# Hash attention and a two-layer MLP: the last quarter of the weight conversion beside the first batch's MLP, the sums product between the halves of the v product, the division in two parts

## The chip, the cores and the metric

The kernel runs on one core of a Trainium2 chip. The metric is the device time of one execution in microseconds (us); each version is judged by the median of several runs. The engines are TensorE (PE; its weight loads are listed as PEld), VectorE (DVE), ScalarE (ACT), GpSimd (POOL) and SyncE (SP), whose queue starts nearly all transfers.

## The reference

The first half is attention with a hash mask, over 4 batches, 8 heads, 768 positions and 64 numbers a head; the second half is an MLP over the 3072 tokens that come out, with 512 to 2048 to 512 features and a leaky activation whose slope `alpha` belongs to the feature.

```python
q_bits = (np.einsum('bhsd,dk->bhsk', q, proj) > 0)      # 6 bits
k_bits = (np.einsum('bhsd,dk->bhsk', k, proj) > 0)
mask = q_bucket[:, :, :, None] == k_bucket[:, :, None, :]
scores = np.where(mask, scale * np.matmul(q, k.transpose(0, 1, 3, 2)), -1e9)
attn = np.exp(scores - np.max(scores, axis=-1, keepdims=True))
attn = attn / (np.sum(attn, axis=-1, keepdims=True) + 1e-09)
x = np.matmul(attn, v)           # then (B,H,S,D) -> (B*S, H*D)
h = x @ w_in
g = np.maximum(h, 0.0) + alpha * np.minimum(h, 0.0)
return g @ w_out
```

The weights come in as 64-bit floats; the kernel rebuilds each one as a 32-bit float from its high and low word.

## The kernel before, in words

`fast_path` does the work; `general_path` behind it is only entered if a flag, worked out in `verdict` from the largest magnitudes seen, says that the fast way was not safe. Every compute instruction goes through `do`, which keeps the order of the program on each engine, so the order in which the code calls its helpers is the order on the queues. Transfers are issued by `nc.sync` and stand on the queue where their waits come due in that order.

**Attention.** Two heads make a pair, so there are 16 pairs; each pair's 768 queries are two units of 384 (CW) columns, so there are 32 units. The unit loop is at L871. In unit u the code calls `scores` three times (parts 0, 1, 2; each makes two blocks of 128 keys by 384 queries for both heads on TensorE, and ScalarE's exponential puts them into one of ten `pt` buffers, L653 and L658). Between the parts stands the work of other stages:

- the sums over keys of unit u: GpSimd adds the first three key blocks (`add_first` L667, `add_third` L670), VectorE the last three and the total (`add_last` L674 to L676, called one unit later);
- the v product of unit u-1 in two halves (`attend`, L686), after parts 0 and 1;
- the sums product of unit u-1 (`totals`, L698): a product with a matrix of ones, which spreads the sum of `accd`. Before the change it follows the second half of the v product. Its output lies in one of the two "mi" banks of PSUM, which the transposes of q and k (`turn`, L614) and the hash (`hash_bits`, L636) use as well;
- the division of unit u-1 (`divide`, L708 to L713), after part 2: a transpose of the sums on VectorE, a reciprocal of the 12 columns that matter, a transpose back, and the product with the v result, which is then stored to `x_s` in DRAM.

**Weight conversion.** 32 pieces (NW) of 128 x 512 numbers, the first 16 (HW) of w_in, the others of w_out. Before, unit u converts piece u. `weight_abs` (ScalarE, L546) is called at the end of the unit before, `weight_parts` (four VectorE operations, L552, L553, L556, L557) after the first half of the v product, `weight_sum` (L577, L582) and `weight_group` after part 1. The group closes four pieces of w_in or two of w_out: four differences on VectorE (L599) that the MLP's scheme needs, and the transfer of the seven blocks to `w_in_s` or `w_out_s` in DRAM. `load_weight` brings the pieces in, three ahead.

**MLP.** Both layers use a scheme with 7 products in place of 8 for a 2 x 2 split (class `Product`). A block of the first layer (`ff1`, 8 a batch) has 7 products of 4 matmuls; a block of the second (`ff2`, 3 a batch) 7 of 16. Each `step` issues one product into a bank "a", "b" or "c"; `keep` has ScalarE copy a partial result out of the bank (tiles `p1`, `p5`, `u1`, `u2`), and `finish` adds two partial results on VectorE (L798) and applies the activation (L803), or for the quadrant "21" copies on ScalarE into `h` and applies it. After "21" of a first-layer block four sums of activations are made (L810), one each for `g` 3, 5, 4 and 6. The order of steps is written out at L937 to L956: 2, 22, 5, 6, 3, 7 of a block, then step 1 of the next, then step 4 of this one. In the profile f_2a is bank a of block 2 of the first layer, z_0b bank b of block 0 of the second.

The differences of the MLP's input, `sums_x` (four GpSimd subtractions of 768 columns, L732), for the first batch are called in unit 16 (HW). `verdict` (small VectorE reductions and four transposes on TensorE, L839 to L853) stands after block 2 of the first batch. The second layer's weights come back from DRAM in the first batch's first-layer blocks, one `wo` tile a block.

Of the kernel before, what the change touches and what calls it, by code (L numbers as in the profile page):

```python
# [403 lines left out]
def fast_path(  # L404
# [71 lines left out]
    prob, accp, accd, av, vsum, sums = {}, {}, {}, {}, {}, {}  # L476
# [40 lines left out]
    HW = NW // 2  # L517

# [12 lines left out]
    def load_weight(i):  # L531
        if i < NW:
            raw[i] = pool.tile([P, 512], moe_w_in.dtype, name=f"raw{i}", tag="raw", bufs=3)
            nc.sync.dma_start(raw[i], piece(i))
# [8 lines left out]
    def weight_abs(i):  # L543
        lo, hi = halves(i)
        wx[i] = pool.tile([P, 512], F32, name=f"wx{i}", tag="wx")
        do(ACT.activation(wx[i], hi.bitcast(F32), AF.Abs))  # L546

    def weight_parts(i):
        lo, hi = halves(i)
        x = wx[i]  # L550
        wr[i] = r = pool.tile([P, 512], F32, name=f"wr{i}", tag="wr", bufs=1)
# [4 lines left out]
        do(DVE.tensor_scalar(r.bitcast(U32), x.bitcast(U32), 0x7F800000, None, op0=ALU.bitwise_and))  # L556
        do(DVE.scalar_tensor_tensor(r, lo, 2.0 ** -52, r, op0=ALU.mult, op1=ALU.mult))  # L557

    def weight_sum(i):
# [26 lines left out]
    def weight_group(i):  # L586
# [113 lines left out]
    def divide(u):  # L700
# [6 lines left out]
        d = pool.tile([P, CW], F32, name=f"dn{u}", tag="dn", bufs=1)  # L707
# [32 lines left out]
    class Product:  # L740
# [20 lines left out]
        def keep(self, bank, what):  # L761
            t = mid.tile([P, CW], F32, name=f"{self.name}{what}", tag=what)[:, : self.width]
# [28 lines left out]
    def ff1(b, i):  # L791
        def finish(c, t, more):
            if more is None:
                h = mid.tile([P, CW], F32, name=f"h{b}_{i}", tag="h")
# [9 lines left out]
            if c == "21":  # L804
                for to, x, op, y in (
# [4 lines left out]
                    do(DVE.tensor_tensor(g_m[to, i], g_m[x, i], g_m[y, i], op=op))  # L810
# [6 lines left out]
    def ff2(b, t):  # L817
        o = {}

        def finish(c, x, more):  # L820
            ch, half = int(c[0]) - 1, slice((int(c[1]) - 1) * DM // 2, int(c[1]) * DM // 2)
            if ch not in o:
                o[ch] = late[0].tile([P, DM], F32, name=f"o{b}_{t}_{ch}", tag=f"o{ch}")
# [45 lines left out]
    for i in range(3):  # L869
        load_weight(i)  # L870
    for u in range(UNITS):  # L871
        pi, g = divmod(u, NCH)
        more = pi + 1 < NPAIR
        scores(u, 0)
        add_first(u)
        if u == 0:
# [24 lines left out]
        if u > 0:  # L901
            attend(u - 1, 1)
            totals(u - 1)
# [3 lines left out]
        if u > 0:  # L907
            divide(u - 1)
        load_weight(u + 3)
        if u == HW:  # L910
# [4 lines left out]
        if u + 1 < NW:  # L915
            weight_abs(u + 1)
# [11 lines left out]
    add_last(last)  # L928
    attend(last, 1)
    now.step(5)  # L930
    totals(last)
    divide(last)
    attn.close()
    late.append(ctx.enter_context(tc.tile_pool(name="late", bufs=2)))
    blocks = [(b, what, n) for b in range(B) for what, count in (("1", NI), ("2", CH)) for n in range(count)]

    for j, (b, what, n) in enumerate(blocks):  # L937
        for st in ((2, 22, 6, 3, 7) if j == 0 else (2, 22, 5, 6, 3, 7)):
            now.step(st)
# [9 lines left out]
        if j == 2:  # L949
            verdict()  # L950
# [35 lines left out]
```

## Time and profile before

| | us |
|---|---|
| runs before | 997.28, 998.04, 999.90 |
| median | 998.04 |
| the profiled execution, its own time | 1000.19 |
| its span, first to last instruction | 998.3 |
| TensorE busy in it | 963.2 (96%) |
| VectorE busy | 605.8 (61%) |
| ScalarE busy | 371.0 (37%) |
| GpSimd busy | 158.5 (16%) |
| mean granted TensorE clock | 0.994 |

The profile is of one execution. A page shows, among others, the span in 40 equal slices of 25 us with each engine's busy share in tenths; the instructions grouped by source line, with the number of instructions, the mean duration in ns and the idle time before them; and who waited for whom ("A <- B: total us, times, longest us"). The stretches give each engine's busy time with its number of instructions between two times, then the granted clock, the share of the transfer engines and GB/s. A row of the timeline has start, duration, engine, line, operation, output and inputs, shape and count; in brackets stands the idle time before it with what ended it. Some durations that the prediction uses, from the groups:

| line | what | count | mean ns |
|---|---|---|---|
| L674, L675, L676 | VectorE's additions for the sums, 768 columns | 32 each | 1260, 1364, 1667 |
| L667, L670 | GpSimd's additions, 768 columns | 32 each | 1939, 1946 |
| L732 | GpSimd's differences of the input, 768 columns | 16 | 2005 |
| L553 | VectorE, shift and exclusive or of a piece | 32 | 1149 |
| L577, L582 | VectorE, the two last operations of a piece | 32 each | 867, 781 |
| L599 | VectorE, differences of a group: w_in, w_out | 16, 32 | 691, 425 |
| L803 | VectorE, activation from h | 32 | 692 |
| L810 | VectorE, sums of activations, 384 columns | 128 | 665 |

### The profile page before, as it was taken

To read this page: it belongs to the slowest core of one execution; us is meant where nothing else is said; L and a number is where in the kernel's file an instruction comes from. 1 tells how busy PE (TensorE), PEld (TensorE's weight loads), DVE (VectorE), ACT (ScalarE), POOL (GpSimd) and SP (SyncE) were. 2 spreads that over 40 slices of the span, in tenths; PEclk is the share of its full clock that TensorE was granted. 3 is DMA by queue.
4 is the path that set the end of the run, shared out by engine and by line. 5 is a ranking of instruction groups with operands and counts; after the bars stand their busy time and mean duration, and the time that the engine had idled before them with its cause. 6 is when DMAs were issued, how large, how long until landed. Compare 5 with 4: busy or idle time off the path is not lost.

```text
span 998.3 us, 12489 instructions
## 1 busy us (share of the span) xinstructions
PE 963.2 (96%) x4741; PEld 594.0 (60%) x4741; DVE 605.8 (61%) x959; ACT 371.0 (37%) x669; POOL 158.5 (16%) x98
## 2 busy tenths in 40 slices
PE   6999999989999998999999999999999999999997
PEld 3444444434444443455788655888656888556886
DVE  3999999999999999766600366500467300665100
ACT  6777676665777664222100122100222000222000
POOL 2333333262333333000300000300000300000000
PEclk9999999998999999999999999999999999999999
DMA  7465756355444431463400133300224200231000
GB/s 199 126 182 143 237 154 179 107 164 157 143 143 143 127 111 53 200 259 110 137 22 22 58 111 99 123 22 21 71 88 155 68 22 22 84 111 37 22 22 24
DMA packets 93316, 106.81 MB, mean 107 GB/s; under 512 B 53296, under 2 KB 79936, under 8 KB 93248
## 3 DMA queue, kind: packets, MB, share of 16 engines
q1 hardware_dynamic: 91680, 105.54, 33.1%
q8 instruction: 39, 0.64, 0.3%
q10 hardware_dynamic: 1568, 0.39, 0.2%
q14 instruction: 29, 0.24, 0.1%
HBM read 78.65 MB, written 27.26 MB: 106 GB/s over the span
## 4 chain that ended last, share of the span: by engine, by line
PE 61%; DVE 35%; ACT 1%; issue 1%; DMA 1%; DVEq 0%; SPq 0%; ACTq 0%
PE z_2a L756 6%; PE z_1a L756 6%; PE z_0a L756 6%; DVE accd L676 5%; DVE accd L675 4%; DVE accd L674 4%; DVE wx L553 3%; PE z_1c L756 3%; PE z_0c L756 3%; PE z_2c L756 3%; DVE wr L577 2%; DVE wr L557 2%; PE f_2a L756 2%; PE f_3a L756 2%; PE f_7a L756 2%; PE f_6a L756 2%
## 5 line engine op out<-in xcount | busy, mean ns | idle before, releaser
L658 ACT ACTIVATE pt<-sc 128x768 f32<-128x768 f32 x192 | 149.9, 813 | 119.8 <-PE sc L653 119.8
L653 PE MATMUL sc<-qT,kT 64*128 64x384 f32 x768 | 157.5, 487 | 0.0
L686 PE MATMUL av<-pt,vn 128*64 128x385 f32 (+1 forms) x768 | 138.1, 495 | 0.0
L667 POOL TENSOR_TENSOR accp<-pt,pt 128x768 f32<-128x768 f32 x32 | 62.0, 1939 | 222.5 <-ACT pt L658 185.2
L686 PEld LDWEIGHTS av<-pt,vn 128*64 128x64 f32 x768 | 49.4, 136 | 72.6 <-issue 72.6
L732 POOL TENSOR_TENSOR x<-x,x 128x768 f32<-128x768 f32 x16 | 31.9, 2005 | 364.0 <-DMA x<-x_s 363.4
L810 DVE TENSOR_TENSOR g<-g,g 128x384 f32<-128x384 f32 x128 | 82.5, 665 | 2.2
L653 PEld LDWEIGHTS sc<-qT,kT 64*128 64x128 f32 x768 | 69.8, 190 | 15.3 <-issue 15.2
L653 PEld LDWEIGHTS <-kb 64*128 64x128 bf16 x384 | 24.4, 94 | 79.3 <-issue 62.7
L653 PE MATMUL sc<-qb,kb 64*128 64x384 bf16 x384 | 64.6, 329 | 5.6 <-ACT pt L658 5.6
L670 POOL TENSOR_TENSOR accp<-accp,pt 128x768 f32<-128x768 f32 x32 | 62.3, 1946 | 39.0 <-ACT pt L658 38.9
L756 PE MATMUL z_2a<-wo,g 128*128 128x256 f32 x256 | 58.0, 379 | 0.5 <-ACT z_2u L763 0.5
L756 PE MATMUL z_1a<-wo,g 128*128 128x256 f32 x256 | 57.9, 379 | 0.0
L756 PE MATMUL z_0a<-wo,g 128*128 128x256 f32 x256 | 57.9, 379 | 0.0
L676 DVE TENSOR_TENSOR accd<-accd,accp 128x768 f32<-128x768 f32 x32 | 53.4, 1667 | 3.3
L803 DVE SCALAR_TENSOR_TENSOR g<-h,alpha 128x384 f32<-128x384 f32 x32 | 22.1, 692 | 54.4 <-ACT h L795 54.4
L756 PEld LDWEIGHTS z_2a<-wo,g 128*128 128x128 f32 x256 | 48.6, 190 | 8.1 <-ACT z_2u L763 0.9
L756 PEld LDWEIGHTS z_0a<-wo,g 128*128 128x128 f32 x256 | 48.6, 190 | 7.5
L756 PEld LDWEIGHTS z_1a<-wo,g 128*128 128x128 f32 x256 | 48.6, 190 | 6.6
L675 DVE TENSOR_TENSOR accd<-accd,pt 128x768 f32<-128x768 f32 x32 | 43.7, 1364 | 3.3
L674 DVE TENSOR_TENSOR accd<-pt,pt 128x768 f32<-128x768 f32 x32 | 40.3, 1260 | 0.0
L639 ACT ACTIVATE qb<-hs,hb 32x384 bf16<-32x384 f32 x64 | 36.7, 574 | 2.2 <-PE hs L636 1.0
(217 smaller groups left out, 1477.1 us busy)
## 6 DMA issues: line engine op xcount, KB each, us to landing
wi<-w_in_s SPq DMA_DIRECT2D x32, 896.0 KB, 4.6
raw<-in_moe_w_in_dram SPq DMA_DIRECT2D x16, 512.0 KB, 4.1
raw<-in_moe_w_out_dram SPq DMA_DIRECT2D x16, 512.0 KB, 3.6
w_in_s<-wsi SPq DMA_DIRECT2D x16, 448.0 KB, 5.4
w_out_s<-wso SPq DMA_DIRECT2D x8, 896.0 KB, 4.4
wo<-w_out_s SPq DMA_DIRECT2D x8, 896.0 KB, 7.4
qn<-in_q_dram SPq DMA_DIRECT2D x32, 192.0 KB, 3.7
vn<-in_v_dram SPq DMA_DIRECT2D x16, 384.0 KB, 4.4
```

Source lines behind the costliest of these rows:

```text
L639: do(ACT.activation(bits["q", pi][D * s : D * s + 32, cols], ps[r], AF.Sign, bias=hb[r]))
L653: do(PE.matmul(sc[:, s, :CW], what["k", pi][r, ks], what["q", pi][r, qs], start=first, stop=not first,))
L658: do(ACT.activation(pt[:, :, :CW], sc[:, :, :CW], AF.Exp, scale=SCALE / DOWN))
L667: do(POOL.tensor_tensor(accp[u], p(u, 0), p(u, 1), op=ALU.add))
L670: do(POOL.tensor_tensor(accp[u], accp[u], p(u, 2), op=ALU.add))
L674: do(DVE.tensor_tensor(accd[u], p(u, 3), p(u, 4), op=ALU.add))
L675: do(DVE.tensor_tensor(accd[u], accd[u], p(u, 5), op=ALU.add))
L676: do(DVE.tensor_tensor(accd[u], accd[u], accp[u], op=ALU.add))
L686: do(PE.matmul(av[u][D * s : D * s + D, :w], nat["v", pi][:, s, kc * D : (kc + 1) * D], prob[u, kc][:, s, :w], start=(kc == 0), stop=(kc = ...
L732: do(POOL.tensor_tensor(x_m[b, to], x_m[b, a], x_m[b, c], op=ALU.subtract))
L756: do(PE.matmul(self.ps[bank], self.left(left, k), self.right(right, k), start=start and k == 0, stop=k == self.nk - 1, skip_group_check=no ...
L810: do(DVE.tensor_tensor(g_m[to, i], g_m[x, i], g_m[y, i], op=op))
```

## The change

- **Conversion.** Pieces 0 to 23 (LW) are converted in attention, in three units of four: unit u takes piece u - u//4 if u % 4 < 3, and every fourth unit takes none. Pieces 24 to 31 are converted one in each first-layer block of the first batch, after that block's step 7; their results (the second half of w_out) go straight into the tiles `wo` 4 to 7 and not through DRAM. `weight_abs` is called in the same unit as the rest, after part 0. The tiles of a piece come from another pool (`mid`), with two `raw` buffers in place of three and one `wx` in place of two; `load_weight` runs two pieces ahead and is called after the group.
- **Sums product.** `totals` is called after the first half of the v product and before part 1 of the scores.
- **Division.** `divide` keeps the transposes and the reciprocal, and is called after `add_third`, before `weight_sum`. The product with the v result and its store become `finish`, called after the second half of the v product.
- **Sums of activations.** In the first batch the four sums of each first-layer block are made by GpSimd in place of VectorE.
- **The rest.** The first batch's `load_x` and `sums_x` move from unit 16 to unit 26; `verdict` moves from after block 2 to after block 8, the first of the second layer; `p5`, `u2`, `h`, `o` and `wso` have one buffer in place of two; the eight `wo` tiles are made at once when the attention's pool is closed.

The core of the diff:

```diff
+    LW = NW - NI
...
             if m == 0:
-                wst[HW + n] = pool.tile([P, NM, DM // 2], F32, name=f"wso{n}", tag="wso")
+                wst[HW + n] = (
+                    pool.tile([P, NM, DM // 2], F32, name=f"wso{n}", tag="wso", bufs=1) if n < NI // 2 else wo[n]
+                )
...
-        else:
+        elif n < NI // 2:
             nc.sync.dma_start(w_out_s[n], w)
...
         do(DVE.transpose(d, r.unsqueeze(2).to_broadcast([P, CW // 32, 32])))
+
+    def finish(u):
+        pi, g = divmod(u, NCH)
+        b, hp = pairs[pi]
         x = pool.tile([P, CW], F32, name=f"x{u}", tag="x")
-        do(DVE.scalar_tensor_tensor(x, av[u][:, :CW], vsum[pi], d, op0=ALU.add, op1=ALU.mult))
+        do(DVE.scalar_tensor_tensor(x, av[u][:, :CW], vsum[pi], den[u], op0=ALU.add, op1=ALU.mult))
         nc.sync.dma_start(x_s[b, hp][:, g * CW : (g + 1) * CW], x)
...
-            t = mid.tile([P, CW], F32, name=f"{self.name}{what}", tag=what)[:, : self.width]
+            t = mid.tile([P, CW], F32, name=f"{self.name}{what}", tag=what, bufs=2 if what in ("p1", "u1") else 1)[:, : self.width]
...
-                    do(DVE.tensor_tensor(g_m[to, i], g_m[x, i], g_m[y, i], op=op))
+
+                    do((DVE if b else POOL).tensor_tensor(g_m[to, i], g_m[x, i], g_m[y, i], op=op))
...
+        w = u - u // 4 if u % 4 < 3 else NW
         scores(u, 0)
         add_first(u)
+        if w < LW and w > 0:
+            weight_abs(w)
...
         if u > 0:
             attend(u - 1, 0)
-        weight_parts(u)
+            totals(u - 1)
+        if w < LW:
+            weight_parts(w)
         scores(u, 1)
         add_third(u)
-        weight_sum(u)
-        weight_group(u)
+        if u > 0:
+            divide(u - 1)
+        if w < LW:
+            weight_sum(w)
+            weight_group(w)
+            load_weight(w + 2)
...
             attend(u - 1, 1)
-            totals(u - 1)
+            finish(u - 1)
...
         scores(u, 2)
-        if u > 0:
-            divide(u - 1)
-        load_weight(u + 3)
-        if u == HW:
+        if u == UNITS - 6:
             load_w(0)
             load_w(1)
             load_x(0)
             sums_x(0)
-        if u + 1 < NW:
-            weight_abs(u + 1)
...
     add_last(last)
+    totals(last)
     attend(last, 1)
     now.step(5)
-    totals(last)
     divide(last)
+    finish(last)
     attn.close()
     late.append(ctx.enter_context(tc.tile_pool(name="late", bufs=2)))
+    wo += [late[0].tile([P, NM, DM // 2], F32, name=f"wo{n}", bufs=1) for n in range(NI)]
...
             if b == 0:
-                wo.append(late[0].tile([P, NM, DM // 2], F32, name=f"wo{n}", bufs=1))
-                nc.sync.dma_start(wo[n], w_out_s[n])
+                if n < NI // 2:
+                    nc.sync.dma_start(wo[n], w_out_s[n])
+                weight_abs(LW + n)
+                weight_parts(LW + n)
+                weight_sum(LW + n)
+                weight_group(LW + n)
+                load_weight(LW + n + 2)
...
-        if j == 2:
+        if j == NI:
             verdict()
```

More of the change, by code (lines that the diff above doesn't have):

```diff
@@ L475, in fast_path @@
     nat, tr, bits = {}, {}, {}
-    prob, accp, accd, av, vsum, sums = {}, {}, {}, {}, {}, {}
+    prob, accp, accd, av, vsum, sums, den = {}, {}, {}, {}, {}, {}, {}
     def load(pi, name, queue=None):
@@ L532, in load_weight @@
         if i < NW:
-            raw[i] = pool.tile([P, 512], moe_w_in.dtype, name=f"raw{i}", tag="raw", bufs=3)
+            raw[i] = mid.tile([P, 512], moe_w_in.dtype, name=f"raw{i}", tag="raw")
             nc.sync.dma_start(raw[i], piece(i))
@@ L544, in weight_abs @@
         lo, hi = halves(i)
-        wx[i] = pool.tile([P, 512], F32, name=f"wx{i}", tag="wx")
+        wx[i] = mid.tile([P, 512], F32, name=f"wx{i}", tag="wx", bufs=1)
         do(ACT.activation(wx[i], hi.bitcast(F32), AF.Abs))
@@ L550, in weight_parts @@
         x = wx[i]
-        wr[i] = r = pool.tile([P, 512], F32, name=f"wr{i}", tag="wr", bufs=1)
+        wr[i] = r = mid.tile([P, 512], F32, name=f"wr{i}", tag="wr", bufs=1)
         do(DVE.tensor_scalar(x, x, HI_MIN, None, op0=ALU.max, op1=ALU.max, accum_out=wmax[:, i : i + 1]))
@@ L706, in divide @@
         r = pool.tile([P, CW // 32], F32, name=f"rc{u}", tag="rc")
-        d = pool.tile([P, CW], F32, name=f"dn{u}", tag="dn", bufs=1)
+        den[u] = d = pool.tile([P, CW], F32, name=f"dn{u}", tag="dn", bufs=1)
         do(DVE.transpose(a, sums[u]))
@@ L793, in finish @@
             if more is None:
-                h = mid.tile([P, CW], F32, name=f"h{b}_{i}", tag="h")
+                h = mid.tile([P, CW], F32, name=f"h{b}_{i}", tag="h", bufs=1)
                 do(ACT.copy(h, t))
@@ L822, in finish @@
             if ch not in o:
-                o[ch] = late[0].tile([P, DM], F32, name=f"o{b}_{t}_{ch}", tag=f"o{ch}")
+                o[ch] = late[0].tile([P, DM], F32, name=f"o{b}_{t}_{ch}", tag=f"o{ch}", bufs=1)
             if more is None:
@@ L868, in fast_path @@
     load(1, "v")
-    for i in range(3):
+    for i in range(2):
         load_weight(i)
```

## The prediction

> **What bounds the kernel now.** I read the page's slices first, then the stretches of the two stages, TensorE's waits, and last the timeline around its longest wait.
>
> ```profile
> PE   6999999989999998999999999999999999999997
> DVE  3999999999999999766600366500467300665100
> POOL 2333333262333333000300000300000300000000
> ```
> TensorE is full everywhere; VectorE is full only in the first sixteen slices, the attention stage.
>
> ```profile
> core 0: us, PE busy (x) PEld busy (x) DVE busy (x) ACT busy (x) POOL busy (x), PEclk, DMA share, GB/s
> 0.00:409.58 409.58, 383.66 (x2505) 169.32 (x2505) 374.65 (x552) 272.96 (x451) 134.84 (x86) 0.99 0.49 147
> 409.58:558.09 148.51, 146.28 (x563) 106.69 (x562) 62.70 (x116) 23.90 (x53) 7.90 (x4) 0.99 0.33 120
> 558.09:702.85 144.76, 144.76 (x561) 106.40 (x561) 57.93 (x97) 24.76 (x55) 7.89 (x4) 1.00 0.22 73
> ```
> Attention, the first batch's MLP, the second's. A batch whose TensorE never idles takes 144.76 us, so the MLP is TensorE's alone. In attention both engines look full, but TensorE hardly waits for VectorE:
>
> ```profile
> PE sm L698 <- DVE accd L676: 7.7, 6, 3.0
> ...
> PE tp_q L614 <- DVE st L708: 2.7, 6, 0.6
> ```
> That makes attention TensorE's too, with VectorE just behind. I measured it by the start of each unit's first score product: 21.74, 33.53, 45.35 us and so on, 11.79 and 11.83 in turn, whenever nothing waits. From unit 1 to the first product after attention is 409.58 - 21.74 = 387.84 us. The floor is 29 units x 11.81 = 342.5, 10.25 for unit 30 (no transposes left; 12.50 less its gaps) and 18.0 for unit 31 and the tail (20.53 less gaps): 370.7. So all of VectorE's load in attention costs 17.1 us, the most that this change can win there: 0.8 in each of units 8, 12 and 16 (a group of four differences), 5.6 in unit 17, 0.7 in 18, 3.7 over units 20 to 28, 2.2 in unit 30, 2.5 in the tail, about 17. The largest piece is this one:
>
> ```profile
> 210.37 8.39 POOL L732 TENSOR_TENSOR x<-x,x 128x768 f32<-128x768 f32 x4
> ...
> 210.73 1.92 DVE L556 TENSOR_SCALAR wr<-wx 128x512 uint32<-128x512 uint32 x1
> 212.68 2.19 DVE L557 SCALAR_TENSOR_TENSOR wr<-raw,wr 128x512 f32<-128x512 uint32 x1
> 214.90 2.19 DVE L577 SCALAR_TENSOR_TENSOR wr<-wx,wr 128x512 f32<-128x512 f32 x1
> ...
> 225.84 1.55 PE L698 MATMUL sm<-accd,ones 128*64 128x384 f32 x4 [3.04 <-DVE accd L676]
> ```
> Four GpSimd subtractions run in a row, and each VectorE operation beside them takes 1.9 to 2.2 us where it takes 0.43 or 0.69 alone: one waits about 1.5 us per GpSimd operation, in turn. The lag reaches TensorE's sums product, which waits 3.04 us.
>
> **What the Trainium skill says.** "SBUF — State Buffer", section "Who interferes with whom": a VectorE operation with two SBUF inputs, or in a 2-port mode, is locked out while GpSimd reads SBUF, and the other way round; one with a single SBUF input, or a tensor_scalar that writes its accumulator, is not. The trace agrees: L577, 0.69 alone, takes 2.06 to 2.19 beside GpSimd; L552 (accumulator) and L713 (one PSUM input) never stretch. "GPSIMD Engine Reference", in the table that reconciles its model with measured numbers: a two-input fp32 add of 2048 columns takes 4497 ns, 2.2 ns a column; 768 columns take 1.81 us here when nothing is in the way, 2.4 a column. "TensorE: Matmul & The Clock Gate", Part 1: the clock is halved after a mostly idle window of 3.4 us. Here the 3.04 us wait brought clock 0.5 for 6.8 us, the 1.97 us wait of the verdict 3.4 us.
>
> **The change, attention.** One unit in four now converts no piece. VectorE's own work per unit, from uncontended rows: three additions 3.0 us, division 1.7, product x 0.53: 5.2. A piece is 3.83 (225.61 to 229.44), a group 2.66 for w_in (103.88 to 106.54), 1.72 for w_out. Before, four units hold 4 x (5.2 + 3.83) + 2.66 = 38.8, and last 48.04: waits for GpSimd's two additions add about 2.2 a unit. After: 4 x 5.2 + 3 x 3.83 + 0.75 x 2.66 + 8.8 = 43.1, against 47.2 of TensorE. On average VectorE has 4 us to spare.
>
> But the sums product moves forward from about +9.1 us in the unit to +4.6 (where scores part 1 starts now), and needs the three additions done. The last exponential lands near +0.8, so they end at +2.9 if VectorE is on time: 1.7 us of slack. A plain converting unit (5.2 + 3.83 + 2.2 = 11.2) keeps that. A unit with a w_in group does not: laying the rows end to end, x ends at +13.4, the next additions start at +1.6 and one meets GpSimd's first addition (+3.5): ready at +6.1, TensorE waits 1.5. There are four such units (4, 9, 14, 20): 6.0 us. Behind a w_out group x ends near +12.5 and the additions at +3.8: nothing. The burst of four subtractions moves to unit 26, and now hits L582 and all three additions: ready near +7.0 in unit 27, 2.4 us of wait and about 1 for the clock (3.4 us at half speed is 1.7, taken at just over half a chance). Unit 30 (group, but only 10.2 us of TensorE) leaves unit 31 2.1 us. With 0.5 for the rest, 12 of the 17.1 us stay: attention gains 5. Bounds: gain 12 if the group units catch up unseen, none if contention falls on the additions everywhere.
>
> **The change, first MLP.** TensorE needs 9.03 us a block. VectorE loses the four sums L810 (0.55 each) to GpSimd. It keeps three additions at 0.59 from start to start and four activations at 0.53: 3.89; a piece adds 3.83, a group every second block 0.86 on average: 8.58. That would fit. But GpSimd's four sums of 384 columns read SBUF just there: three can start as soon as the activation of "22" is done, which is when the piece starts. No row shows 384 columns. Half of the 1.5 us is 0.75 per operation; the price above gives 0.84 in all; below nothing is excluded, since a lock only takes time. Laid out: 0.3 on L553 (the first sum hides mostly behind L552), 0.7 on L556, 0.7 on L557, and 0.4 for the fourth sum on the next block's activation: 2.1 a block (bounds 0.9 and 3.0). VectorE then needs 10.7 us a block against 9.03 and is the bound. From the first product after attention: first addition of "22" at 5.75, eight blocks of 8.58 less the 2.24 of a next block, plus 16.4: the last activation of ff1, behind piece 31 and its group, ends at 88.6. TensorE wants it for the end of z_0b, at 76.1. Loss 12.5 us. TensorE runs at most half a block ahead of VectorE (p5, u2, h have one buffer), so about 6 us of it fall together before z_0b: a clock drop, +2. Sum +14.5.
>
> Costed at nothing: single buffers for p5, u2, h, o in later batches (p5 is free 1.8 us after a block's last product and needed 5.2 after; o's copy-out of 2.0 us has over 13); the SP queue (a raw load waits for L582, but stands behind the wi load that is due; wi's load of 4.6 us has 7 before its block, 1.4 in the lagging state; if that goes, the rest of the 4.6 appears per block); ScalarE's Abs, moved behind two exponentials (it hides beside the additions); w_out of four pieces no longer passing through DRAM. The verdict's wait moves from after block 2 to after z_0: it cost 4.8 us including the clock, and I leave it so, +-2.
>
> Sum: -5 + 14.5 = +9.5. The profiled execution (span 998.3, its own time 1000.19) would become 1009.7; the median of the runs, 998.04, is 2.15 below it: 1007.5.
>
> **Rivals.** (1) Attention wins nearly everything (12 us) while the MLP still loses 14.5: 1000.5. For it: VectorE's 4 us to spare in four units. Against: TensorE's new deadline half a unit earlier. (2) The other side, faster: GpSimd's sums fall beside operations that don't contend (L552, the PSUM additions), at 0.9 us a block. VectorE needs 9.5; the loss is 3.1 with no clock drop, and attention gains 10: 991. The loss is 7.8 times the wait a block less 3.9: with attention's gain at 5 the sign turns at 1.1 us a block, with 10 at 1.8. Against: the burst at 210 us, where each operation waited in turn. (3) Worse: 3.0 a block (loss 20, clock 3) and no gain in attention: 1021. That the change does not do what it says I exclude: in the instruction streams of the changed program the sums product stands between the halves, and 24 pieces stand in attention.
>
> **Chances.** Forecast 1003 to 1014: 0.55; (1) 0.15; (2) 0.15; (3) 0.15. A measurement can tell 0.3%, 3 us. Faster (below 995): most of (2) and a little of (1), 0.17. Same: the rest of (1), 0.13. Slower: 0.70. Range: 992 to 1018, cutting the far halves of (2) and (3).
>
> **What would show it.** The changed profile should have: unit starts 11.8 apart except after units 4, 9, 14, 20 (sums product waiting for accd about 1.5) and in unit 27; ff1 blocks of the first batch over 10 us with VectorE full; L553, L556, L557 stretched there; a wait of several us in z_0b for the activation; later batches at 144.8. I am wrong if GpSimd's 384-column sums leave L556 and L557 at 0.43 and 0.69, or if the sums product waits in every unit.

## The result, and the profile after

| | before | after |
|---|---|---|
| runs, us | 997.28 to 999.90 (4) | 1012.92 to 1015.51 (4) |
| median, us | 997.95 | 1014.01 |
| the profiled execution, its own time | 1000.19 | 1015.51 |
| its span | 998.3 | 1013.7 |
| mean granted TensorE clock | 0.994 | 0.991 |

The changed kernel is slower: the ratio is 1.0159, with a 95% interval of 1.0138 to 1.0179. In the line numbers of the changed kernel the sums product is L701, its input is made at L677 to L679, GpSimd's additions are L670 and L673, the differences of the input L739; the operations of a piece are L553, L554, L557, L558, L580, L585 and its group L602; the division is L711 to L714 and L720; the MLP's products are L763, the copies out of a bank L770, the additions L805, the activation L810 and the sums of activations L818.

The same three rows of slices as before, now of the changed kernel:

```profile
PE   6999989999999898999699999999999999999997
...
DVE  3777777876968787799710166600366400565100
...
POOL 2322322232232632243510000300000300000000
```

VectorE is less busy in attention than it was (mostly 7 and 8 tenths where it had 9), and TensorE has lost a little more there all the same. VectorE's 9s now stand in slices 18 and 19, the first batch's first layer; TensorE has 9s there too, and a 6 in slice 20, where the second layer begins.

The stretches of attention (from unit 1), of the first batch's MLP and of the second's say how much:

```profile
core 0: us, PE busy (x) PEld busy (x) DVE busy (x) ACT busy (x) POOL busy (x), PEclk, DMA share, GB/s
22.27:412.79 390.52, 370.95 (x2429) 162.91 (x2428) 304.91 (x466) 254.99 (x417) 122.43 (x66) 0.99 0.45 127
412.79:573.57 160.78, 149.03 (x562) 107.15 (x561) 87.81 (x151) 28.77 (x62) 40.64 (x36) 0.98 0.31 108
573.57:718.33 144.76, 144.76 (x562) 106.40 (x561) 57.80 (x97) 24.70 (x55) 7.90 (x4) 1.00 0.22 73
```

Attention takes 390.52 us against 387.84 before (+2.7), the first MLP, from its first product behind attention to the same product of the next batch, 160.78 against 148.35 (+12.4), the second batch 144.76 as before. With 0.5 us before unit 1 and -0.2 at the end that is the 15.4 us by which the span grew. TensorE's waits in the changed kernel (total, times, longest):

```profile
PE sm L701 <- DVE accd L679: 14.4, 6, 4.4
...
PE z_0b L763 <- DVE g L810: 5.0, 1, 5.0
PE f_7c L763 <- ACT f_7p L770: 2.2, 1, 2.2
...
PE f_5c L763 <- ACT f_5p L770: 1.2, 1, 1.2
PE vd L852 <- DVE top L847: 1.1, 1, 1.1
```

Six waits of the sums product, 14.4 us, stand where the kernel before had six of 7.7 in all. They lie in units 5, 10, 15, 21 (behind a group of w_in), 27 (behind the four subtractions) and 31; every other unit from 1 to 29 is 11.79 or 11.83 long, except 12.23 for unit 26, and unit 30, which has no transposes, takes 10.22. The wait of z_0b for the activation is new. A half-clock stretch of 3.41 us lies in unit 10, and two longer ones follow the two longest waits (the clock is the last column but two):

```profile
core 0: us, PE busy (x) PEld busy (x) DVE busy (x) ACT busy (x) POOL busy (x), PEclk, DMA share, GB/s
346.44:353.27 6.83, 5.07 (x20) 1.95 (x24) 3.27 (x5) 0.97 (x2) 1.63 (x2) 0.50 0.00 0
500.04:506.87 6.83, 5.75 (x14) 4.59 (x15) 1.41 (x4) 0.00 (x0) 5.59 (x4) 0.50 0.00 0
```

TensorE worked 5.07 and 5.75 us of them at half speed, so by estimate half of that, 2.5 and 2.9 us, is lost on top of the waits.

**The longest unit.** VectorE around the four subtractions in unit 26 and the start of unit 27 (339.12), then GpSimd, then TensorE:

```profile
334.57 1.61 DVE L712 TENSOR_SCALAR rc<-st 128x12 f32<-128x12 f32 x1
...
336.98 1.49 DVE L580 SCALAR_TENSOR_TENSOR wr<-wx,wr 128x512 f32<-128x512 f32 x1
338.51 2.18 DVE L585 SCALAR_TENSOR_TENSOR wso<-raw,wr 128x512 uint32<-128x512 uint32 x1
...
341.14 2.05 DVE L677 TENSOR_TENSOR accd<-pt,pt 128x768 f32<-128x768 f32 x1
343.29 2.38 DVE L678 TENSOR_TENSOR accd<-accd,pt 128x768 f32<-128x768 f32 x1
345.78 2.37 DVE L679 TENSOR_TENSOR accd<-accd,accp 128x768 f32<-128x768 f32 x1
```
```profile
334.47 1.68 POOL L673 TENSOR_TENSOR accp<-accp,pt 128x768 f32<-128x768 f32 x1 [1.90 <-ACT pt L661]
336.10 8.75 POOL L739 TENSOR_TENSOR x<-x,x 128x768 f32<-128x768 f32 x4
344.82 2.51 POOL L670 TENSOR_TENSOR accp<-pt,pt 128x768 f32<-128x768 f32 x1
```
```profile
348.20 1.55 PE L701 MATMUL sm<-accd,ones 128*64 128x384 f32 x4 [4.42 <-DVE accd L679]
```

GpSimd has six operations in a row without a gap, from 334.47 to 347.33, and VectorE six two-input or tensor_scalar operations beside them, each 0.8 to 1.5 us longer than alone (0.69 for L580 and L585, 0.96 for an addition). Even L712, a tensor_scalar of 12 columns that takes 0.17 us alone, took 1.61. The last addition ends 9.0 us into unit 27, and TensorE's sums product starts right behind it.

**The first layer of the first batch.** VectorE in block 3, between two pieces of the conversion:

```profile
441.20 0.68 DVE L553 TENSOR_SCALAR_CACHE_REDUCE wx<-wx 128x512 f32<-128x512 f32 x1
...
441.93 0.72 DVE L554 TENSOR_SCALAR wx<-wx 128x512 uint32<-128x512 uint32 x1
442.68 1.10 DVE L557 TENSOR_SCALAR wr<-wx 128x512 uint32<-128x512 uint32 x1
443.82 1.37 DVE L558 SCALAR_TENSOR_TENSOR wr<-raw,wr 128x512 f32<-128x512 uint32 x1
445.22 0.69 DVE L580 SCALAR_TENSOR_TENSOR wr<-wx,wr 128x512 f32<-128x512 f32 x1
...
447.67 1.06 DVE L810 SCALAR_TENSOR_TENSOR g<-f_3p,alpha 128x384 f32<-128x384 f32 x1
...
450.88 0.68 DVE L553 TENSOR_SCALAR_CACHE_REDUCE wx<-wx 128x512 f32<-128x512 f32 x1
...
462.40 0.68 DVE L553 TENSOR_SCALAR_CACHE_REDUCE wx<-wx 128x512 f32<-128x512 f32 x1
```
```profile
441.37 3.27 POOL L818 TENSOR_TENSOR g<-g,g 128x384 f32<-128x384 f32 x3 [2.74 <-DVE g L810]
447.31 1.00 POOL L818 TENSOR_TENSOR g<-g,g 128x384 f32<-128x384 f32 x1 [2.67 <-DVE g L810]
```

From one L553 to the next are 9.68 us without a group, and 11.52 in the following block, which has one. VectorE has no gap in either, and TensorE needs 9.03 a block. L554, L557, L558 and one activation are 0.29, 0.67, 0.68 and 0.44 us longer than alone: 2.1 a block, while GpSimd's four sums run.

### The profile page after: what moved, and what is told of

Same layout as the page of the kernel before. It is cut to its first block, busy times and chain, and to the rows that moved or that the text cites. A ratio compares the mean times of both kernels' runs of the same rounds, so it can differ in the third digit from the quotient of the medians.

```text
span 1013.7 us, 12460 instructions
## 1 busy us (share of the span) xinstructions
PE 966.1 (95%) x4741; PEld 595.4 (59%) x4741; DVE 566.9 (56%) x927; ACT 371.7 (37%) x669; POOL 184.9 (18%) x130
## 4 chain that ended last, share of the span: by engine, by line
PE 77%; DVE 15%; ACT 5%; issue 3%; DMA 1%; SPq 0%; ACTq 0%; DVEq 0%
PE sc L656 10%; PE av L689 9%; PE z_2a L763 5%; PE z_1a L763 5%; PE z_0a L763 5%; ACT pt L661 3%; PE z_0c L763 3%; PE z_2c L763 3%; PE z_1c L763 3%; PE hs L639 2%; PE f_0a L763 2%; PE sm L701 2%; PE f_5a L763 2%; PE f_6a L763 2%; PE f_7a L763 2%
## 5 line engine op out<-in xcount | busy, mean ns | idle before, releaser
L670 POOL TENSOR_TENSOR accp<-pt,pt 128x768 f32<-128x768 f32 x32 | 63.6, 1986 | 187.9 <-ACT pt L661 187.9
L739 POOL TENSOR_TENSOR x<-x,x 128x768 f32<-128x768 f32 x16 | 31.6, 1983 | 275.3 <-DMA x<-x_s 274.6
L673 POOL TENSOR_TENSOR accp<-accp,pt 128x768 f32<-128x768 f32 x32 | 54.0, 1688 | 86.2 <-ACT pt L661 79.3
L818 DVE TENSOR_TENSOR g<-g,g 128x384 f32<-128x384 f32 x96 | 60.7, 653 | 1.7
L763 PE MATMUL z_0a<-wo,g 128*128 128x256 f32 x256 | 58.1, 379 | 1.0 <-DVE g L810 1.0
L763 PE MATMUL z_2a<-wo,g 128*128 128x256 f32 x256 | 58.0, 379 | 0.5 <-ACT z_2u L770 0.5
L763 PE MATMUL z_1a<-wo,g 128*128 128x256 f32 x256 | 57.9, 379 | 0.0
L763 PEld LDWEIGHTS z_0a<-wo,g 128*128 128x128 f32 x256 | 48.6, 190 | 8.8 <-DVE g L810 1.4
L763 PEld LDWEIGHTS z_2a<-wo,g 128*128 128x128 f32 x256 | 48.6, 190 | 8.1 <-ACT z_2u L770 0.9
L763 PEld LDWEIGHTS z_1a<-wo,g 128*128 128x128 f32 x256 | 48.6, 190 | 6.6
L818 POOL TENSOR_TENSOR g<-g,g 128x384 f32<-128x384 f32 x32 | 33.5, 1056 | 65.4 <-DVE g L810 47.9
L677 DVE TENSOR_TENSOR accd<-pt,pt 128x768 f32<-128x768 f32 x32 | 31.7, 989 | 20.2 <-ACT pt L661 20.2
L580 DVE SCALAR_TENSOR_TENSOR wr<-wx,wr 128x512 f32<-128x512 f32 x32 | 42.2, 1319 | 0.3
L810 DVE SCALAR_TENSOR_TENSOR g<-h,alpha 128x384 f32<-128x384 f32 x32 | 20.5, 641 | 38.3 <-ACT h L802 38.3
L701 PE MATMUL sm<-accd,ones 128*64 128x384 f32 x128 | 27.1, 503 | 14.4 <-DVE accd L679 14.4
```

Source lines behind the costliest of these rows:

```text
L580: do(DVE.scalar_tensor_tensor(r, x, -1.0 if turned else 1.0, r, op0=ALU.mult, op1=ALU.subtract if turned else ALU.add,))
L670: do(POOL.tensor_tensor(accp[u], p(u, 0), p(u, 1), op=ALU.add))
L673: do(POOL.tensor_tensor(accp[u], accp[u], p(u, 2), op=ALU.add))
L677: do(DVE.tensor_tensor(accd[u], p(u, 3), p(u, 4), op=ALU.add))
L701: do(PE.matmul(sums[u][D * s : D * s + D], ones, accd[u][:, s], start=True, stop=True))
L739: do(POOL.tensor_tensor(x_m[b, to], x_m[b, a], x_m[b, c], op=ALU.subtract))
```

## The experiments

Each was timed together with the kernel before on one chip: e1 to e4 beside 29 runs of it (median 998.85), e5 to e8 beside 10 (998.03), e9 and e10, on another chip, beside 15 (999.42). The ratio is to these runs. "Attention" is from unit 1's first score product to the MLP's first product behind attention's last, "first MLP" from there to the same product of the second batch; both are from one profiled execution of each kernel. Before has 387.84 and 148.35, the floors are 370.7 and 144.76. In every kernel the second and third batches took 144.76.

| kernel | median us | ratio to before, interval | attention | first MLP |
|---|---|---|---|---|
| after | 1014.01 | 1.0159 (1.0138 to 1.0179) | 390.5 | 160.8 |
| e1 | 1018.42 | 1.0201 (1.0179 to 1.0224) | 390.4 | 164.0 |
| e2 | 1001.89 | 1.0034 (1.0025 to 1.0044) | 378.6 | 160.6 |
| e3 | 1000.36 | 1.0016 (1.0008 to 1.0025) | 389.8 | 146.8 |
| e4 | 1007.84 | 1.0090 (1.0071 to 1.0108) | 383.5 | 160.7 |
| e5 | 1002.97 | 1.0038 (1.0026 to 1.0051) | 378.1 | 161.4 |
| e6 | 989.89 | 0.9909 (0.9890 to 0.9928) | 378.7 | 146.2 |
| e7 | 1004.92 | 1.0055 (1.0035 to 1.0075) | 392.0 | 148.4 |
| e8 | 1022.09 | 1.0226 (1.0208 to 1.0243) | 413.9 | 147.0 |
| e9 | 988.98 | 0.9900 (0.9881 to 0.9918) | 378.5 | 146.3 |
| e10 | 999.87 | 1.0011 (1.0002 to 1.0020) | 373.9 | 160.8 |

My theory after the result: the first MLP loses its 12 us because pieces and contention make VectorE the bound there; attention loses because the sums product is wanted half a unit earlier, and because the four subtractions meet that deadline. Rivals: GpSimd's sums are a trade that costs or gains much by itself; the wait moves about and has no single cause.

**e1: the sums of activations back on VectorE.** The changed kernel with one line undone:

```diff
-                    do((DVE if b else POOL).tensor_tensor(g_m[to, i], g_m[x, i], g_m[y, i], op=op))
+                    do(DVE.tensor_tensor(g_m[to, i], g_m[x, i], g_m[y, i], op=op))
```

> The changed kernel with one thing undone: the four sums of activations of the first batch are VectorE's again; the eight late pieces stay in its first-layer blocks. Theory [...]: VectorE's block was 8.6 us of own work plus 2.1 of waiting for GpSimd; now it is 8.6 plus four sums of 0.53, 10.7 again. The time stays within 3 us of the changed kernel's 1014. Rival (GpSimd really takes 17 us off VectorE): 1031.

Measured 1018.42, 4.4 us more than after; the first MLP is 3.2 longer, and z_0b waits 8.2 us in place of 5.0. The expectation of no more than 3 us was missed by a little, the rival's 1031 by far. The theory holds for the blocks themselves: from one L553 to the next VectorE takes 9.72 us without a group and 11.56 with one, where the changed kernel takes 9.68 and 11.52. The last of these steps is another matter, 13.74 us (483.22 to 496.96):

```profile
471.67 0.68 DVE L553 TENSOR_SCALAR_CACHE_REDUCE wx<-wx 128x512 f32<-128x512 f32 x1
...
483.22 0.68 DVE L553 TENSOR_SCALAR_CACHE_REDUCE wx<-wx 128x512 f32<-128x512 f32 x1
...
491.28 1.59 DVE L810 SCALAR_TENSOR_TENSOR g<-f_7u,alpha 128x384 f32<-128x384 f32 x1
492.79 2.17 DVE L805 TENSOR_TENSOR f_7p<-f_7p,f_7u 128x384 f32<-128x384 f32 x1
495.00 2.04 DVE L810 SCALAR_TENSOR_TENSOR g<-f_7p,alpha 128x384 f32<-128x384 f32 x1
496.96 0.67 DVE L553 TENSOR_SCALAR_CACHE_REDUCE wx<-wx 128x512 f32<-128x512 f32 x1
```
```profile
490.55 8.16 POOL L739 TENSOR_TENSOR x<-x,x 128x768 f32<-128x768 f32 x4 [87.65 <-DMA x<-x_s]
```

Without sums of its own GpSimd starts the next batch's four subtractions at once, and they stretch three operations of VectorE that take 0.55 to 0.62 us alone, 4.0 us in all. In the changed kernel the sums hold GpSimd, and the subtractions come at 502.16, behind VectorE's last activation. Up to the start of that step the two kernels are level: the L553 before it starts 70.8 us into the first MLP in both (483.22 here, 483.58 there). So the 32 sums of 0.55 us, 17.6 us of VectorE's time, came back nearly whole as VectorE's waits, 2.1 us a block; what e1 loses is where another burst falls. The Trainium skill says of this in "Perfetto Trace Analysis", section "Optimizing Scalar/DVE Operations", that moving work between these two engines "might not help"; here it made VectorE's blocks faster by 0.04 us each, and no more.

**e2: the sums product and the division in their old places.** The changed kernel, with the order of the attention undone and the pieces left where the change put them:

```diff
             attend(u - 1, 0)
-            totals(u - 1)
...
         add_third(u)
-        if u > 0:
-            divide(u - 1)
...
             attend(u - 1, 1)
-            finish(u - 1)
+            totals(u - 1)
...
         scores(u, 2)
+        if u > 0:
+            divide(u - 1)
+            finish(u - 1)
...
```

> The changed kernel with the sums product and the whole division put back where they were (after the second half of the v product, and after the scores' last part); the conversion stays as changed. Theory (the early place of the sums product makes TensorE wait, 19.8 us over its floor in attention): four units with w_in groups lose their 9.3 us of waiting, unit 27 some of its 7.0, the tail some of its 3.3; 10 to 14 us less, 1000 to 1004. Rival (VectorE's load and GpSimd's locks set the waits wherever the product stands): 1012 to 1016.

Measured 1001.89, as the theory had it. Attention falls by 11.9 us to 378.6; units 5, 10, 15 and 21 are clean. Of the six waits of the sums product two are left:

```profile
PE sm L701 <- DVE vs L695: 3.0, 1, 3.0
PE sm L701 <- DVE accd L679: 2.8, 1, 2.8
```

What is left over the floor is 7.9: unit 27 with 3.2, the tail with the wait of 2.8 and a half clock. So the new places of the sums product and the division together are worth 11.9 us of loss in attention. The two were not moved apart; that it is the sums product is read from TensorE's waits, which are its own.

**e3: no late pieces.** The kernel leaves out the second half of w_out and multiplies by the first half twice.

```diff
...
-        do(DVE.tensor_reduce(top[:, 2:3], wmax, axis=mybir.AxisListType.X, op=ALU.max))
+        do(DVE.tensor_reduce(top[:, 2:3], wmax[:, :LW], axis=mybir.AxisListType.X, op=ALU.max))
...
             if b == 0:
-                if n < NI // 2:
-                    nc.sync.dma_start(wo[n], w_out_s[n])
-                weight_abs(LW + n)
-                weight_parts(LW + n)
-                weight_sum(LW + n)
-                weight_group(LW + n)
-                load_weight(LW + n + 2)
+                nc.sync.dma_start(wo[n], w_out_s[n % (NI // 2)])
```

> The changed kernel without the conversion of pieces 24 to 31, which is left out: the four converted tiles of w_out stand in for the other four, by a transfer each. Theory (the late pieces make VectorE the bound of the first batch's blocks): blocks at 9.03 us, the first MLP at 146 us where the changed kernel takes 160.8, 999 to 1001 in all. Rival (the sums on GpSimd come late for the second layer): a wait of some us before z_0 stays, 1006 or more.

Measured 1000.36, the first MLP 146.84, as the theory had it; z_0b does not wait. GpSimd still makes the sums, as the row of this kernel's first MLP shows (42.03 us, against 8 in a batch without them):

```profile
411.84:558.68 146.84, 144.59 (x561) 105.64 (x560) 43.31 (x79) 24.38 (x54) 42.03 (x36) 1.00 0.33 122
```

So the pieces cost 160.78 - 146.84 = 13.9 us where they stand, the half-clock stretch included; GpSimd's sums cost nothing that shows where no piece stands beside them. Over a batch that never waits this MLP has 146.84 - 144.76 = 2.1 us, against 148.35 - 144.76 = 3.6 before. Of TensorE's waits in it 1.4 are the verdict's (1.1 and 0.3) and 0.9 is f_2a's for a transfer of wi, so the verdict in its new place costs at most the 1.5 us that e6 has below, where hardly anything else waits.

**e4: the four subtractions one at a time.** The changed kernel with one subtraction each in units 19, 23, 27 and 31, the loads in unit 17.

```diff
...
-        if u == UNITS - 6:
+        if u == HW + 1:
             load_w(0)
             load_w(1)
             load_x(0)
-            sums_x(0)
+        if u > HW and u % 4 == 3:
+            sums_x(0, (u - HW) // 4)
```

> The changed kernel with GpSimd's four differences of the first batch's input taken apart: one in each of units 19, 23, 27 and 31, which convert no piece, in place of four in a row in unit 26. Theory (the row of four holds VectorE's additions up, and TensorE waits 4.4 us and runs 6.8 us at half clock): each single one hides in a unit with 4 us to spare, unit 27 falls from 18.8 to 11.8; 1007. Rival (each one costs its 1.5 us at the sums product of its own unit): 1012 to 1014.

Measured 1007.84, as expected. Unit 27 is clean, attention 383.5: 7.0 us less. The waits of the other units stay, and so does unit 26 with 12.23 us:

```profile
PE sm L701 <- DVE accd L679: 10.0, 5, 3.1
```

So the burst in its new place costs 7.0, wait and clock, all of it in unit 27.

**e5: e2 and e4 together.** Both edits, shown above.

> The changed kernel with both: the sums product and the division back in their old places, and the four differences one each in units 19, 23, 27 and 31. With the product back alone the median was 1001.9, with 7.9 us over the floor in attention: 3.2 in unit 27, the rest in the tail. Theory: unit 27 is clean, 998 to 999.5. Rival (VectorE's load still shows): 1001 or more.

Measured 1002.97, no better than e2: the theory's number was missed and the rival's came true, although unit 27 is clean as the theory had it. Attention is 378.1, because the loss stands in the tail now. GpSimd, and what VectorE did beside it (in this kernel the differences are L740):

```profile
381.92 2.52 POOL L740 TENSOR_TENSOR x<-x,x 128x768 f32<-128x768 f32 x1
```
```profile
380.42 2.36 DVE L677 TENSOR_TENSOR accd<-pt,pt 128x768 f32<-128x768 f32 x1
382.88 2.37 DVE L678 TENSOR_TENSOR accd<-accd,pt 128x768 f32<-128x768 f32 x1
```

The fourth subtraction, in unit 31, meets the last additions: the sums product waits 4.3 us in place of 2.8, and a half-clock stretch of 6.8 us follows.

**e10: e5 with the subtractions one place earlier.** Units 15, 19, 23 and 27 in place of 19, 23, 27 and 31.

> The kernel of e5 (1002.97 us; sums product and division in their old places, the four differences apart) with the differences in units 15, 19, 23 and 27 in place of 19, 23, 27 and 31, their loads one unit pair earlier. Theory (in e5 the fourth difference in unit 31 made the tail wait 4.26 us and cost a half-clock stretch): the tail wait returns to about 2.9 us, unit 27 stays clean, 998 to 1000 us. Rival (the differences only move the wait to another unit, whichever follows them): 1002 to 1003, with a new wait in one of the units 16, 20, 24 or 28.

Measured 999.87, the theory's number. Attention is 373.9, only 3.2 over the floor: the tail's wait of 2.8 and 0.2 in unit 23. That settles e5: the miss was the fourth subtraction in the tail. And it says what attention gains when eight pieces leave it, the order stays as it was and the subtractions are spread: 387.8 - 373.9 = 13.9 us. With the subtractions in one row it was 387.8 - 378.6 = 9.2 (e2). The first MLP loses 160.8 - 148.4 = 12.4, and the kernel ends level with before.

**e7: the subtractions apart in the kernel before.** Its burst stood in unit 16; here one each in units 15, 19, 23 and 27, and nothing else is changed.

> The kernel before with one thing changed: the four differences of the first batch's input one each in units 15, 19, 23 and 27, in place of four in a row in unit 16. Theory (VectorE is full in attention before, so it pays for each of the four wherever it stands, and only the long wait with its half clock goes): 995 to 997. Rival (the row alone cost the 5.6 us of unit 17): 992 to 993.

Measured 1004.92: slower than before, which neither theory had (6.9 us by the medians; in the profiles attention is 4.2 longer, but the profiled execution of before is 2.2 above its median and that of e7 0.4 below). TensorE's waits in this kernel:

```profile
PE tp_q L614 <- DVE st L708: 8.7, 6, 2.1
...
PE sm L698 <- DVE accd L676: 4.7, 5, 2.0
```

The waits for the division's transpose grow from 2.7 to 8.7 us: units 16, 20, 24 and 28 are 15.8, 15.5, 15.5 and 14.2 us long, and three of them carry a half-clock stretch of 3.4 us. With 32 pieces each subtraction made its own wait, where the burst made one. But units 15, 19, 23 and 27 are units that close a group in this kernel, the fullest kind; a unit without a group was not tried. In e6 and e9 below, with 28 pieces, a subtraction in a unit with a piece but no group (27; 17 and 26) leaves the next unit 0.2 to 0.3 us longer, one in a unit with a group (19 of e6) 1.8. Spreading paid in units without a piece (e4, e10), and not here.

**e8: the new order in the kernel before.** Sums product and division as in the change, with all 32 pieces in attention.

```diff
...
             attend(u - 1, 0)
+            totals(u - 1)
         weight_parts(u)
         scores(u, 1)
         add_third(u)
+        if u > 0:
+            divide(u - 1)
...
             attend(u - 1, 1)
-            totals(u - 1)
+            finish(u - 1)
...
         scores(u, 2)
-        if u > 0:
-            divide(u - 1)
...
```

> The kernel before with the second part of the change alone: the sums product after the first half of the v product, the division in two parts. All 32 pieces stay in attention, one a unit. Theory (the additions must now be ready 4.6 us into a unit in place of 9.1, and VectorE is late in nearly every unit): TensorE waits 0.5 to 1.5 us in most units, 1012 to 1030. Rival (the order costs only where a group or a row of differences stands): 1000 to 1008.

Measured 1022.09, attention 413.9, within the range of the theory. But the waits do not stand in most units; their places are the rival's, behind groups and the row of differences:

```profile
PE sm L698 <- DVE accd L676: 27.7, 12, 2.8
```

Twelve waits, in units 4, 8, 12, 16 (w_in groups, up to 2.8 us), 17, then every second unit from 20 to 28 (w_out groups, 1.8), 30 (2.5) and the tail; the units between take 11.8, and five of them 12.0. Seven half-clock stretches go with them, which by half of TensorE's busy time in them cost an estimated 13 us; before has one in attention, of 3. So the new order costs 26.1 us of attention with 32 pieces, and 11.9 with 24 (after against e2): each time mostly behind the groups.

**e6: a version sized by these results.** Old order; 28 pieces in attention (none in units 7, 15, 23 and 31); the subtractions one each in units 15, 19, 23 and 27, two of which have a piece; four pieces in the MLP, in every second block of the first layer; the sums of activations on VectorE.

```diff
...
-    LW = NW - NI
+    LW = NW - 4
...
-        w = u - u // 4 if u % 4 < 3 else NW
+        w = u - u // 8 if u % 8 < 7 else NW
...
+        if u in (15, 19, 23, 27):
+            sums_x(0, u // 4 - 3)
...
+                if n % 2 == 0:
+                    i = LW + n // 2
+                    weight_abs(i)
+                    weight_parts(i)
+                    weight_sum(i)
+                    weight_group(i)
+                    load_weight(i + 2)
...
```

> A version sized to the engines. The sums product and the division in their old places; 28 pieces in attention (seven units of eight), 4 in the first batch's blocks 0, 2, 4 and 6; the sums of activations on VectorE in all batches; the four differences one each in units 15, 19, 23 and 27. Theory: a pair of blocks costs VectorE 12.0 + 3.83 + 0.86 = 16.7 us against TensorE's 18.1, so the first MLP takes 146 to 148; attention has 90.7 us of VectorE against 94.5 in eight units and ends 4 to 7 us above its floor: 982 to 986. Rival (VectorE's margin is too thin in either stage, and waits return): 990 to 998.

Measured 989.89, ratio 0.9909 (0.9890 to 0.9928): faster than both kernels, by 8 us against before, though not the 982 to 986 of the theory; it lies at the edge of the rival's 990 to 998, and the rival's waits are there in attention. Its attention and its first MLP:

```profile
21.58:400.24 378.66, 367.82 (x2429) 161.17 (x2428) 344.82 (x497) 258.76 (x422) 133.54 (x66) 1.00 0.48 141
400.24:546.47 146.23, 144.70 (x563) 105.75 (x562) 78.13 (x152) 26.23 (x57) 7.97 (x4) 1.00 0.33 117
```

The MLP part came as reckoned: TensorE busy 144.70 of 146.23, and four pieces cost nothing that shows. Two blocks ask VectorE for 2 x (3.89 + 4 x 0.55) + 3.83 + 0.86 = 16.9 us on average, 17.7 with a group of 1.72, where TensorE takes 18.1. Attention kept 8.0 over its floor: 1.8 in unit 20, 0.8 in unit 22, 1.4 in unit 30, a wait of 2.85 in the tail, and the rest in a few tenths. Its profile has no half-clock stretch before the last 6 us, that of before has two; but runs of before whose mean clock was 0.998 or 0.999 still took 997, so most of the 8 us is not the clock.

**e9: e6 with a lighter tail.** No pieces in units 12, 21, 30 and 31, the subtractions in units 12, 17, 21 and 26.

> The kernel of e6 (989.89 us; 28 pieces in the attention, four in the first MLP, old places of sums product and division), with no pieces in units 12, 21, 30 and 31 in place of 7, 15, 23 and 31, and the four differences in units 12, 17, 21 and 26 in place of 15, 19, 23 and 27. In e6 the attention still held waits of 1.15 us in unit 20, 1.4 in unit 30 and 2.85 in the tail. Theory (a wait stands where VectorE has no slack left in its unit, and the tail has none because units 30 and 31 carry pieces): the waits of unit 30 and of the tail go, unit 20's shrinks, 985 to 988 us, attention near 374. Rival (a unit without a piece in the middle is needed there as well, and the pieces moved forward only move the wait): about 990, attention near 378.

Measured 988.98; the interval of its ratio, 0.9881 to 0.9918, overlaps with that of e6 for the most part. The tail's wait is gone and unit 20 is clean, but unit 30 keeps 1.5, units 8 and 12 now hold 0.8 each and units 19 and 28 1.8 each: attention 378.5. The rival was right: with 28 pieces there is too little slack, and the wait moves.

## Why the prediction was right, and which steps failed

The direction, the places and the range were right (1014.0 within 992 to 1018; the likeliest number, 1007.5, was 6.5 us too low, and 1014.0 is the upper edge of the likeliest band). The direction came from the first MLP alone: attention was forecast with the wrong sign. By its steps:

**The first MLP (14.5 predicted, 12.4 measured): right in mechanism and size.** The prediction put 2.1 us of contention on L553, L556, L557 (here L554, L557, L558) and the next block's activation, at 0.75 an operation; the trace has 2.1, on just these. Blocks were to take 8.58 + 2.1 with a group every second one; the two blocks above have 9.68 and 11.52, mean 10.6 against 10.7. The loss was to fall half before and half at z_0b, with one clock drop of 2: TensorE waits 1.18, 0.38 and 2.21 in blocks 5, 6 and 7, 1.00 in z_0a and 4.95 in z_0b, 9.7 in all, and the clock takes 2.9. e3 gives the whole step directly: 13.9 us for 14.5. The rest is the verdict, which I left at its old price: by e3 against before the first MLP gained 1.5 there, inside my +-2. Its wait for `top` fell from 2.0 to 1.1 us and no half clock came with it. That the sums on GpSimd save VectorE nothing follows from this sum too (2.1 us of waits against four sums of 0.53), and e1 shows it.

**Attention (-5 predicted, +2.7 measured): the step that failed.** I said 12.0 of the 17.1 us would stay; 19.8 are there. No place was wrong; the sizes were:

| term | predicted | measured |
|---|---|---|
| units 5, 10, 15, 21, behind w_in groups | 6.0 | 9.4 (1.75 three times, 4.1 in unit 10) |
| the burst, unit 27 | 3.4 | 7.0 |
| unit 31 and tail | 2.1 | 3.0 |
| the rest (unit 26, in e4 as well) | 0.5 | 0.4 |

*The burst.* I let it hit one operation of the piece and the three additions. It hit two more: L580, stretched by 0.8, and L712, by 1.4 through GpSimd's L673 just ahead of the four; together 2.2. The sums were ready at 9.0 us into unit 27, not 7.0. I also took the clock as 3.4 us at half speed with half a chance; the wait of 4.42 brought 6.8 us, an estimated 2.5 lost. e4 takes all of it away: 7.0.

*Unit 10.* I gave all four units the same wait of 1.5. Three have 1.55. Before unit 10 VectorE has one more small operation (L695, 0.15 us, due once per pair), and its second addition waits 0.46 for an exponential. So the sums come 0.6 us later, TensorE waits 2.22, and that wait brought 3.4 us of half clock, which the 1.55 did not.

*What the mean hid.* The 4 us that VectorE gets to spare in four units are real: with the order as before the lighter attention gains 9.2 with the subtractions in one row (e2) and 13.9 with them spread (e10), on either side of the 12 of rival (1). The new order takes this back: the sums must be ready 4.5 us earlier in the unit, and the unit behind a w_in group has no slack ahead of that deadline. I had this against rival (1), and undersized it: 12.0 us staying, where 19.8 stayed.

**Costed at nothing.** Single buffers: in later batches nothing shows (144.76). In the first batch's MLP one does show, in the waits of f_5c, f_6c and f_7c for ScalarE's copy into the one `p5`: 3.8 us. It is not a cost on top: VectorE, the bound, still holds `p5`, and without this wait the same time would fall due in z_0b (argued, not run). wi waits 0.3 and 0.4 in two blocks. ScalarE's Abs does not hide beside the additions, as I had it. Before, VectorE waits for it in unit 0 alone; now it waits about 0.5 us in most units that convert a piece, units 4, 9, 14 and 20 with their w_in groups among them:

```profile
61.26 0.69 DVE L553 TENSOR_SCALAR_CACHE_REDUCE wx<-wx 128x512 f32<-128x512 f32 x1 [0.51 <-ACT wx L547]
```

From there VectorE has no gap until the additions that TensorE waits 1.55 us for in unit 5, so up to a third of such a wait can be this term. No run moves Abs alone.

**The clock.** The Trainium skill, "TensorE: Matmul & The Clock Gate", Part 1, describes the activity window as 3413 ns long and free-running. The stretches here are 3.41 and 6.83 us (10.24 behind the wait of 8.2 in e1), and in each profile they start whole multiples of 3.413 us apart: in the changed kernel at 138.23, 346.44 and 500.04, which is 61 and 45 windows. Both agree. The page halves the clock after an idle window; "mostly idle" in the prediction is my reading of it, for the waits that did it here, from 1.8 us (e7) up, are often shorter than a window. Nor does the same wait always do it: 2.22 in unit 10 did, 2.21 in f_7c did not; the verdict's 2.0 did before, and the same 1.97 did not in e8, whose first MLP is 147.0 in place of 148.4; the 4.42 of unit 27 brought 6.83 us in the changed kernel and 3.41 in e3. A window that runs on its own would do this; no run tests it by itself. It also spreads the runs of one kernel: the 15 runs of before beside e9 and e10 go from 997.27 to 1000.31, with mean clocks between 0.993 and 0.998.

What stays open: whether a version exists in which attention holds more than 24 pieces without waits, and how much of the loss behind the w_in groups is Abs. e6 and e9 show two distributions of 28 with 8 us over the floor each, in different units.

## What to carry to other kernels

An engine's spare time counts in front of the deadline it serves. Lay its operations end to end in the units around the heaviest one, with every shared lock in the row, the smallest operations too, before believing a mean; a consumer that is moved half a unit forward can take back more than the load that was removed. Work that is moved to another stage should be sized by that stage's slack (here four pieces, 1.2 us left in every two blocks, and not eight), and work that is handed from VectorE to GpSimd by the waits that it hands back (here all of it), and by what GpSimd would do in its place.

## What had not been expected of the hardware

- A GpSimd addition of 384 columns took 0.99 to 1.18 us, where half the price of 768 columns (1.67 to 1.83 with nothing in the way) would be 0.84 to 0.92.
- The wait that GpSimd put on VectorE was no shorter for a short operation: 1.44 us for a tensor_scalar of 12 columns (1.61 against 0.17), 1.42 for an addition of 768. The Trainium skill, "SBUF — State Buffer", section "Who interferes with whom", says of a VectorE operation in a 2-port mode, which a tensor_scalar can enter, that whichever engine issues first blocks the other for the whole instruction. That fits: L712 ends at 336.18, GpSimd's L673 at 336.15. Beside GpSimd's operations of 384 columns the wait was at most 0.68.
- Four waits of about 2 us in four places cost more than one burst that makes a single wait of 3 (e7, 6.9 us slower by the medians); part of it lies in three half-clock stretches of 3.4 us in place of one of 6.8.
- The next batch's subtractions, which no edit had moved, cost VectorE 4.0 us in e1, because GpSimd had become free to start them earlier.
